# Reordering the hand-written queue at the end of the first pair: last values and output-matrix part five ahead of the norm's multiply and the placing, and the second pair's token sums in order of need

## The chip, the cores and the metric

One core of a Trainium2 chip. The metric is the device time in microseconds (us) of one execution. The kernel is all float32. TensorE (PE) runs the matmuls, VectorE (DVE), ScalarE (ACT) and GpSimd (POOL) the elementwise work, and SyncE (SP) issues most of the DMAs; ACT issues a few.

## The reference, cut to what matters

The input x has 8 sequences of 4096 tokens with 192 features. First a causal convolution over 7 tokens, with softmax weights per head, and then a gated feed-forward network with an RMS norm in front:

```
out = einsum('hk,bskhg->bshg', softmax(weight), windows_of(x))   # 8 heads, 7 taps
x   = out.reshape(32768, 192)
xn  = x / sqrt(mean(x * x, -1) + 1e-6) * rms_g
g   = xn @ w_gate                    # 192 -> 1536
out = (g * sigmoid(g) * (xn @ w_val)) @ w_out   # 1536 -> 192
```

## The kernel before, in words

The tokens are taken in 32 "pairs" of 1024 tokens (two groups g of T = 512). Pair 0 is different from the other 31. It is done with plain products, while the weights are still being converted from their stored form. Pairs 1 to 31 are done with fewer, larger combinations (sums of tokens and sums of weights) and follow one fixed list, `ORDER`. The change concerns only the seam between pair 0 and pair 1, which is passed once.

The program order of each engine is written by hand: the kernel asks for a manual schedule, so each engine executes its instructions in the order in which the Python code emits them, and waits by semaphore for what it needs. For pair 0 the emission is steered by two tables of single letters, each of which advances one generator by a step:

- `s`: one SiLU of a gate product on ACT (L1011). It reads a PSUM bank of half 0 (`ps0` to `ps3`) and writes one of five work tiles.
- `v`: one value step on DVE (L1018). It multiplies a product in a bank of half 1 (`ps4` to `ps7`) by the SiLU tile into `ht`, and gives the bank free.
- `O`: a step of converting an odd part (one, three, five) of the output matrix `wo_sb`. The first step of a part is three DVE operations (L287, L291, L294), the second three ACT operations (L298, L299, L302), the third one DVE operation (L304) and two on POOL (L310, then L311, which writes `wo_sb`). `o` is the same for the even parts.
- `n`: a step of the norm of pair 1. The last of its five steps is a multiply of 128x1536 elements on POOL (L499), which writes `yn`.
- `t`: the placing of pair 1, `place(1)`: eight DMAs that write `yn` to a scratch tensor `xd` in DRAM (L635), four of them issued by SP and four by ACT.
- `w`: sums of the input weights for the later pairs, on POOL (L350, L346).

`START` is played at once, next to pair 0's input products (L1001). `LATER` holds pairs of a time and a letter. Its steps are put into one queue with everything else of pair 0's second stage. The times are only places in that queue (100 is one 512-column product), and the queue is emptied in their order.

The other entries of the queue, with `base` the end of the input products and `c = base + 200`:

- `outer(0, ...)`: pair 0's output products (L1041), 192 instructions on 64 rows of the array each, half 0 and half 1 running beside each other; each shows as two records in the trace. They run over the two token groups g, for each over four blocks j of 128 tokens, and contract over 12 parts f of the hidden features. For g = 0, blocks 0 and 1 lie in banks `ps0` and `ps4`, blocks 2 and 3 in `ps2` and `ps6`. For g = 1 half 0 goes into `ps1` first.
- `part_tap(2, k, j)`: the convolution of pair 2, in PSUM: tap 0 on ACT (L437), taps 1 to 6 on DVE (L445). The three thirds j use banks `ps1`, `ps5` and `ps3` as accumulators; the last tap writes to SBUF and frees the bank. The first two thirds are interleaved, 12 instructions on DVE; the eleventh is the last to read `ps1`.
- `fetch(1)`: four DMAs by SP that read pair 1's tokens from `xd` into `xb` (L648); then `norm(2)` (its square on ACT is L461, its first reduction on DVE L472), and `load(3)`.
- `x_sum(i)`: eleven sums of tokens (L670, DVE) from `xb` into `xc` for pair 1, with sums that build on others.

Pair 1 then begins with products of `xc` and of sums of weights (L757).

Of the kernel before, what the change touches and what calls it, by code (L numbers as in the profile page):

```python
# [19 lines left out]
def kernel(  # L20
# [673 lines left out]
    def put(at, do):  # L694
        heapq.heappush(line, (at, next(tick), do))
# [291 lines left out]
    def plain(hts):  # L987


        groups = [(u, g, f) for u in range(NU) for g in (1, 0) for f in range(NF)]  # L990
        groups[0 : 2 * NF] = [(0, g, f) for f in range(NF) for g in (1, 0)]
        held = {}

        def products():
            for u, g, f in groups:
                if len(hts) <= u:
                    hts.append(big.tile([P, 2, NF, T], F32, name="ht"))
                bks = held[u, g, f] = [free[h].pop(0) for h in range(2)]
                for k in range(KP):
                    for h in range(2):  # L1000
                        nc.tensor.matmul(  # L1001
                            out=bank(h, bks[h])[:], lhsT=wf[u][HALF[h], k * NF + f, :],
                            rhs=xb[HALF[h], g, k, :], start=(k == 0), stop=(k == KP - 1),
                            skip_group_check=True,
                        )
                yield

        def silus():
            for i in groups:
                sg = tiles.pop(0)  # L1010
                nc.scalar.activation(out=sg[:], in_=bank(0, held[i][0])[:], func=AF.Silu)  # L1011
                held[i].append(sg)
                yield

        def values():
            for u, g, f in groups:
                *bks, sg = held.pop((u, g, f))
                nc.vector.tensor_tensor(  # L1018
                    out=hts[u][:, g, f, :], in0=bank(1, bks[1])[:], in1=sg[:], op=ALU.mult
                )  # L1020
                tiles.append(sg)
                for h in range(2):
                    free[h].append(bks[h])
                yield

        return products(), silus(), values()
# [89 lines left out]
    def done(it):  # L1116
# [8 lines left out]

    START = (
        "XxxxxxXDdDdDTDdadTbTaTfbTakTakTakTkbkKkKkKkbkbfpoffpfsicpsvivOpsipisvicpsvpvwsicwpvs"
        "iwpvscwpsiwvpisvicpsvovpwispvswcipvwspsiwOvpsiwvipsvvpswopsvcpsvOnovoOpsonvOpsnoOvnopsoOn"
    )
    LATER = (  # L1130
        (55, "O"), (60, "t"), (163, "s"), (170, "O"), (200, "v"), (294, "v"),
        (463, "w"), (564, "w"), (664, "w"), (764, "w"), (864, "w"), (964, "w"), (1064, "w"),
        (1164, "w"), (1264, "w"),
    )
# [9 lines left out]
    p, sl, v = plain(hts)  # L1144
# [37 lines left out]
    for j in range(len(SIDE)):  # L1182
        put(c + 240 + 700 * (j // 2), functools.partial(part_tap, 2, 0, j))
        for k in range(1, K):
            at = c + 250 + 100 * k + 50 * j if j < 2 else c + 960 + 80 * k
# [3 lines left out]
    later(place(2), c + 2450)  # L1189
    xat = [c + i for i in (1660, 1730, 2060, 2130, 2200, 2270, 2290)]  # L1190
    xat += [c + i for i in (2360, 2370, 2380, 2390)]
    for i, at in enumerate(xat):
        put(at, functools.partial(x_sum, i))
    later(out_sums(), *[base + 2600 + 60 * i for i in range(4 * NM)])
    emit(float("inf"))
# [48 lines left out]
```

## Time and profile before

| | |
|---|---|
| median of 3 runs | 2607.96 us (2606.99 to 2608.02) |
| the profiled execution: its own time | 2610.66 us |
| the profiled execution: span from first to last instruction | 2608.7 us |
| mean granted TensorE clock | 0.997 |
| busy share of the span | PE 99%, DVE 87%, POOL 80%, ACT 62% |
| PE's idle time in the whole run, first 42 us apart | 4.5 us in 4 waits, of which 2.9 us in one |

The page counts an engine as busy while one of its instructions runs. The granted clock is the share of TensorE's full clock that the chip allowed it: at 0.50 a matmul takes twice its time and still counts as busy. Names such as `ps` stand for a whole family of buffers; where the text speaks of `ps1`, the number is from the order of the program.

### The profile page before, as it was taken

What the parts mean: (1) busy time and instruction counts of PE and PEld (TensorE: products, weight loads), DVE (VectorE), ACT (ScalarE), POOL (GpSimd) and SP (SyncE); (2) the same over time, 40 slices, a digit from 0 to 9 for tenths busy, and PEclk for the clock granted to TensorE, in tenths of its full rate; (3) what the DMA queues carried; (4) which work ended last, traced back from release to release, by engine and by line L of the source; (5) the groups of instructions that cost most, each with busy time, mean ns of one, the idle gap of its engine ahead of it and who ended that gap; (6) DMA issues with size and microseconds to landing.
All of it is one profiled execution on the core that took longest, in us unless ns stands there. A gap on an engine that the chain in (4) does not pass through costs nothing.

```text
span 2608.7 us, 60700 instructions
## 1 busy us (share of the span) xinstructions
PE 2575.5 (99%) x23794; PEld 1869.1 (72%) x23794; DVE 2272.6 (87%) x3617; ACT 1618.6 (62%) x2967; POOL 2081.1 (80%) x1693
## 2 busy tenths in 40 slices
PE   6999999999999999999999999999999999999999
PEld 3677777777777766777777777777777777777776
DVE  8988888988888988898888889888888888888875
ACT  5375556765556765557655567655577555676554
POOL 3878788877888777888788887778887888887776
PEclk9999999999999999999999999999999999999999
DMA  6313321323312223213233122232132332232210
GB/s 144 56 39 57 63 47 42 63 39 63 63 35 54 51 51 63 50 39 63 39 63 63 37 52 51 51 63 52 38 61 40 62 63 42 47 60 41 50 38 13
DMA packets 512603, 137.36 MB, mean 53 GB/s; under 512 B 484284, under 2 KB 486844, under 8 KB 512189
## 3 DMA queue, kind: packets, MB, share of 16 engines
q1 hardware_dynamic: 509068, 132.80, 26.7%
q8 instruction: 186, 3.05, 0.5%
q10 hardware_dynamic: 3248, 0.69, 0.1%
q14 instruction: 101, 0.83, 0.1%
HBM read 83.87 MB, written 49.55 MB: 51 GB/s over the span
## 4 chain that ended last, share of the span: by engine, by line
PE 97%; DVE 2%; DMA 0%; ACT 0%; issue 0%; DVEq 0%; SPq 0%; ACTq 0%
PE ps L757 62%; PE ps L889 33%; PE ps L1041 1%; PE ps L1001 1%; DVE xc L304 0%; DMA x<-in_x_dram 0%; DVE ht L1018 0%; DVE y L406 0%; DVE y L421 0%; DVE y L394 0%; PE ps L595 0%; DVE wf L319 0%; ACT xb L615 0%; DVE xc L314 0%; DVE xc L287 0%
## 5 line engine op out<-in xcount | busy, mean ns | idle before, releaser
L757 PE MATMUL ps<-xc,wf 64*128 64x512 f32 x4960 | 1250.0, 592 | 0.0
L757 PEld LDWEIGHTS ps<-xc,wf 64*128 64x128 f32 x4960 | 755.4, 186 | 308.8 <-issue 66.2
L757 PE MATMUL ps<-xb,wf 64*128 64x512 f32 x2480 | 710.4, 589 | 0.0
L801 POOL TENSOR_TENSOR ht<-ht,tile 128x512 f32<-128x512 f32 x298 | 378.8, 1280 | 277.1 <-ACT tile L794 275.1
L708 ACT ACTIVATE tile<-ps 128x512 f32<-128x512 f32 (+1 forms) x677 | 391.0, 593 | 319.5 <-PE ps L757 190.1
L708 ACT ACTIVATE tls<-ps 128x512 f32<-128x512 f32 (+1 forms) x656 | 376.1, 589 | 314.9 <-PE ps L889 192.7
L757 PEld LDWEIGHTS ps<-xb,wf 64*128 64x128 f32 x2480 | 391.9, 187 | 143.6 <-issue 30.7
L708 ACT ACTIVATE ps<-ps 128x512 f32<-128x512 f32 (+1 forms) x651 | 366.9, 578 | 54.0 <-PE ps L889 39.0
L917 POOL TENSOR_TENSOR early<-ht 128x512 f32<-128x512 f32 x279 | 379.4, 1365 | 4.9
L889 PE MATMUL ps<-ht,wo_sb 128*32 128x128 f32 (+2 forms) x5208 | 318.6, 380 | 0.0
L445 DVE SCALAR_TENSOR_TENSOR ps<-xh,tp,ps 128x512 f32<-128x512 f32 x450 | 312.0, 745 | 1.2
L801 POOL TENSOR_TENSOR ht<-ht,tls 128x512 f32<-128x512 f32 x198 | 251.6, 1277 | 76.2 <-ACT tls L794 74.6
L781 DVE TENSOR_TENSOR tile<-ps,tile 128x512 f32<-128x512 f32 x366 | 250.1, 687 | 62.8 <-PE ps L757 56.1
L889 PEld LDWEIGHTS ps<-ht,wo_sb 128*32 128x32 f32 x5208 | 234.2, 110 | 81.5 <-POOL ht L801 23.5
L889 PE MATMUL ps<-ht,x 128*32 128x128 f32 (+2 forms) x4464 | 250.7, 379 | 0.0
L917 POOL TENSOR_TENSOR ht<-ht 128x512 f32<-128x512 f32 x186 | 248.2, 1351 | 0.0
L794 ACT ACTIVATE tile<-tile 128x512 f32<-128x512 f32 x366 | 228.2, 629 | 12.5 <-DVE tile L781 12.5
L889 PEld LDWEIGHTS ps<-ht,x 128*32 128x32 f32 x4464 | 184.6, 110 | 61.1
L781 DVE TENSOR_TENSOR ht<-ps,tile 128x512 f32<-128x512 f32 x322 | 219.1, 681 | 0.1
L781 DVE TENSOR_TENSOR ht<-ps,tls 128x512 f32<-128x512 f32 x298 | 202.7, 680 | 0.0
L889 PE MATMUL ps<-early,x 128*32 128x256 f32 (+2 forms) x3348 | 196.0, 379 | 0.0
L781 DVE TENSOR_TENSOR tls<-ps,tls 128x512 f32<-128x512 f32 x254 | 173.9, 685 | 25.1 <-PE ps L757 23.6
(129 smaller groups left out, 3176.9 us busy)
## 6 DMA issues: line engine op xcount, KB each, us to landing
xb<-xd SPq DMA_DIRECT2D x124, 384.0 KB
xd<-yn SPq DMA_DIRECT2D x244, 96.0 KB
xh<-in_x_dram SPq DMA_DIRECT2D x192, 105.0 KB
out_dram<-o_sb SPq DMA_DIRECT2D x122, 96.0 KB
out_dram<-o_sb SPq DMA_DIRECT2D x62, 128.0 KB
xh<-in_x_dram SPq DMA_DIRECT2D x56, 98.4 KB
out_dram<-o_sb SPq DMA_DIRECT2D x122, 32.0 KB
ht<-in_moe_w_gate_dram SPq DMA_DIRECT2D x12, 192.0 KB
```

What stands on the lines that cost most here:

```text
L445: nc.vector.scalar_tensor_tensor(out=dst, in0=xk, scalar=w, in1=at, op0=ALU.mult, op1=ALU.add)
L708: nc.scalar.activation(out=dst, in_=src, func=AF.Copy, scale=float(s))
L757: nc.tensor.matmul(out=self.new(v, h, True) if first else self.old(v, h), lhsT=wf[self.u][HALF[h], WAT[i], :], rhs=x_op(XOP[i])[HALF[h]], ...
L781: nc.vector.tensor_tensor(out=self.hv(v) if h else t[:], in0=self.old(v, h), in1=t[:], op=plus(s))
L794: nc.scalar.activation(out=t[:], in_=src[:], func=AF.Silu)
L801: engine[eng].tensor_tensor(out=self.hv(v), in0=src, in1=t[:], op=ALU.mult)
L889: nc.tensor.matmul(out=self.bank(b)[i * Q : (i + 1) * Q, at : at + n], lhsT=left, rhs=cols, start=fresh, stop=True, skip_group_check=True, ...
L917: engine[eng].tensor_tensor(out=dst, in0=a, in1=b, op=op)
L1001: nc.tensor.matmul(out=bank(h, bks[h])[:], lhsT=wf[u][HALF[h], k * NF + f, :], rhs=xb[HALF[h], g, k, :], start=(k == 0), stop=(k == KP - 1 ...
L1041: nc.tensor.matmul(out=bank(h, bks[h])[:, w : w + D], lhsT=hts[f // NF][HALF[h], g, f % NF, j * P : (j + 1) * P], rhs=wo_sb[HALF[h], f, :] ...
```

## The change

Two tables are edited; no instruction is added or removed on any engine.

```
-        ...isvicpsvpswopsvcpsvOnovoOpsonvOpsnoOvnopsoOn"
+        ...isvicpsvpswopsvcpsvOnovoOpsonvOpsnoOvnopsoO"
     LATER = (
-        (55, "O"), (60, "t"), (163, "s"), (170, "O"), (200, "v"), (294, "v"),
+        (30, "s"), (35, "v"), (40, "O"), (45, "v"), (50, "O"), (55, "n"), (60, "t"),
         (463, "w"), (564, "w"), (664, "w"), ...
...
     xat += [c + i for i in (2360, 2370, 2380, 2390)]
-    for i, at in enumerate(xat):
+    for i, at in zip((0, 1, 7, 2, 3, 5, 6, 10, 8, 9, 4), xat):
         put(at, functools.partial(x_sum, i))
```

(The first line of `START` is left out above, and the front of its second line is shortened.)

The order that results on each engine:

- DVE: the last two value steps come before L304 of part five; before, they came after it. The eleven token sums keep their places as a group, and inside it stand as 0, 1, 7, 2, 3, 5, 6, 10, 8, 9, 4.
- ACT: the last SiLU comes before the three operations of part five and the four DMA issues; before, it came after them. The square and tap 0 of pair 2 stay behind the DMA issues.
- POOL: L310 and L311 of part five come before L499; before, they came after it.
- PE and SP: the same order as before.

More of the change, by code (lines that the diff above doesn't have):

```diff
@@ L1127 @@
         "XxxxxxXDdDdDTDdadTbTaTfbTakTakTakTkbkKkKkKkbkbfpoffpfsicpsvivOpsipisvicpsvpvwsicwpvs"
-        "iwpvscwpsiwvpisvicpsvovpwispvswcipvwspsiwOvpsiwvipsvvpswopsvcpsvOnovoOpsonvOpsnoOvnopsoOn"
+        "iwpvscwpsiwvpisvicpsvovpwispvswcipvwspsiwOvpsiwvipsvvpswopsvcpsvOnovoOpsonvOpsnoOvnopsoO"
     )
     LATER = (
-        (55, "O"), (60, "t"), (163, "s"), (170, "O"), (200, "v"), (294, "v"),
+        (30, "s"), (35, "v"), (40, "O"), (45, "v"), (50, "O"), (55, "n"), (60, "t"),
         (463, "w"), (564, "w"), (664, "w"), (764, "w"), (864, "w"), (964, "w"), (1064, "w"),
```

## The prediction

> **What bounds the kernel now.** I read the busy row and the chain first: PE is busy for 99% of the span and the chain that ended last is 97% PE. A change that moves no matmul can only touch PE's waits or its clock. So next came PE's waits (engine, line, releaser; total, times, longest):
>
> ```profile
> PE ps L534 <- ACT early L402: 17.6, 2, 16.9
> PE ps L595 <- ACT xc L588: 5.6, 1, 5.6
> PE ps L1041 <- DVE ht L1018: 2.9, 1, 2.9
> ```
>
> The first two lie ahead of pair 0's products and aren't touched. The third is the seam that the change edits. The timelines of DVE, POOL and ACT around it (start, length, engine, line):
>
> ```profile
> 104.54 1.06 DVE L291 TENSOR_SCALAR xc<-xc 128x384 uint32<-128x384 uint32 x1
> 105.52 1.17 DVE L294 TENSOR_SCALAR xc<-tls 128x384 uint32<-128x384 uint32 x1
> 106.62 3.14 DVE L304 SCALAR_TENSOR_TENSOR xc<-tls,xc 128x384 uint32<-128x384 uint32 x1
> 109.68 0.68 DVE L1018 TENSOR_TENSOR ht<-ps,tile 128x512 f32<-128x512 f32 x1
> ...
> 106.44 2.94 POOL L499 TENSOR_TENSOR yn<-y,s 128x1536 f32<-128x1536 f32 x1
> 109.30 1.32 POOL L310 TENSOR_TENSOR xc<-xc,tls 128x384 f32<-128x384 f32 x1
> ...
> 107.16 0.54 ACT L302 ACTIVATE tls<-tls 128x384 f32<-128x384 uint32 x1
> 109.41 2.89 ACTq L635 DMA_DIRECT2D xd<-yn  x4
> 112.35 0.60 ACT L1011 ACTIVATE tile<-ps 128x512 f32<-128x512 f32 x1 [4.65 <-POOL wf L350]
> 112.84 1.90 ACT L437 ACTIVATE ps<-xh,tp 128x512 f32<-128x512 f32 x3
> ...
> 113.58 6.67 DVE L445 SCALAR_TENSOR_TENSOR ps<-xh,tp,ps 128x512 f32<-128x512 f32 x10
> 120.16 1.40 DVE L445 SCALAR_TENSOR_TENSOR y<-xh,tp,ps 128x512 f32<-128x512 f32 x2
> ```
>
> L304 takes 3.14 us because it meets L499 on POOL (beside an idle POOL it took 0.54 at 88.29). The value step behind it starts at 109.68; PE, which wants that step's bank `ps6`, stands from 107.51 to 110.41. The stall costs more than its length; stretches of PE (length, PE busy and records, clock, DMA share and rate):
>
> ```profile
> 107.50:109.60 2.10, 0.01 (x1) 1.00 0.00 0
> 109.60:110.40 0.80, 0.00 (x0) 0.51 0.00 0
> 110.40:116.40 6.00, 5.99 (x38) 0.50 0.61 131
> 116.40:123.00 6.60, 6.60 (x84) 1.00 0.77 175
> ```
>
> From 109.6 to 116.4 half the clock is granted: six microseconds of matmuls do three microseconds' work. The seam costs 2.9 + 3.0 = **5.9 us**, 0.23% of the run; this is the most that the change can win. About 0.2% (5.2 us) is what a measurement of this kernel can tell from no change.
>
> [...] 2.1 us of standing were enough, and half clock lasted 6.8 us. [...] L291 takes 0.36 at 95.46 and 1.06 at 104.54 beside POOL. [...] Here the SiLU at 112.35 stood 4.65 us behind DMA issues.
>
> **The change, part by part, on the profiled execution's clock.**
>
> *Values first.* Up to L294 nothing ahead changes; L294 ends at 106.69. The value step for `ps6` has its SiLU (ended 102.73) and can start at about 106.6; at 0.68 it ends at 107.3. PE wants the bank at 107.36 (the matmul before it starts at 107.19, and they come every 0.16). So this stall goes, with 0.06 to spare. Bounds: 0 to 0.5 us of stall, if DVE slips by half an operation; I take none. The second value step ends at 107.9; its SiLU moves to about 103.3 on an idle ACT, right after the last L1001 product (ended 103.17). That costs nothing.
>
> *Part five before the multiply.* L302 on ACT ends at 107.70 as before, so L310 starts at 107.7 and takes 1.0. L304, now third on DVE, starts at 107.8 and meets L310 as the one at 102.24 did (1.17): it ends at about 109.1. L311 needs it: 109.1 to 110.1. Only then comes L499, alone at 2.9: 110.1 to **113.0**, where it ended at 109.38: 3.6 us later. Bounds 112.6 (L302's end and 1.0 + 1.0 + 2.9) to 113.6. `wo_sb` part five is first needed by matmul record 143, at 107.36 + 86 x 0.081 = 114.3: met with 4 us to spare.
>
> *What stands behind the multiply.* The placing needs `yn`. ACT's four issues took from 109.41 to the next instruction at 112.35, 2.93 us; now 113.0 to 115.9. Behind them in ACT's order is L437, tap 0 of pair 2. It started at 112.84 with the SiLU in front; that is gone, so it starts at about 116.1. The first L445 on DVE followed the first L437's start by 0.74: now 116.8, where it was 113.58. The bank `ps1` is read last by the eleventh L445, which ran from 120.16 to 120.90: now 123.4 to **124.1**.
>
> *When PE wants that bank.* Counting the 384 records of L1041, the first matmul into `ps1` is number 187; it ran at 124.03, 3.1 us after the bank was free, so no wait shows. The one at the old stall is number 57. Without stall and at full clock, 187 comes at 107.36 + 130 x 0.081 = **117.9**. Its bank is free at 124.1. So PE stands for 6.2 us at a new place, and starts record 187 at about 124.2, where it started at 124.03. Both halves of the gain are eaten: PE came 6.1 us earlier and the bank 3.2 us later, against 3.1 us of slack.
>
> *The clock after it.* A stand of 6.2 us is longer than the one that halved the clock. If half clock ends as it did, about 6 us after the restart, 3.0 us are lost behind record 187, which were lost ahead of it before. The price has bounds: 0 if the clock holds, 3.4 if a half-clock stretch of 6.8 us falls wholly on work. I take 3.0.
>
> *Token sums and the rest.* DVE's chain, the fetch, the square and the reductions all shift by about 3.2 us: the last sum ended at 137.7 and now ends at 140.9. PE reaches pair 1 at 124.2 + 16.4 (140.44 less 124.03) + 3.0 = 143.6, where it was 140.1 to 140.4, so the sums are there in any order. Reordering them costs nothing and gains nothing while PE is that late. If the clock held, PE would come at 140.6 and the order would hide up to 0.3 us. SP issues its four placing DMAs and the fetch behind the same multiply: fetch from 116.31 to about 119.9; it took until about 125 to move and would until 129, ahead of the first sum at 133.2. POOL's weight sums start 1.3 us later than their 111.66 and are wanted by later units of pair 1. Nothing of these ends last.
>
> Sum: 124.2 against 124.03 is +0.2, and the half clock moved behind the bank +3.0: **+3.2 us**, on 2608.7 of span and 2610.66 of the profiled execution's own time. The runs' median is 2.7 us under that time; on it I put +3.1: 2611.1.
>
> **The rivals.**
>
> *Half clock only in the new kernel.* The shown runs are 2 to 3.7 us under the profiled execution's time. If this is because their 2.9 us stand, falling otherwise in time, doesn't halve the clock, record 187 starts there at about 121.0 and the new 6.2 us stand costs +3.2 and +3.0: +6.2, 2614.2, slower by 0.24%. It decides once the half-clock loss after exceeds the loss before by 2.0 us. [...] Against it: three runs within 1.0 us don't look like a loss of 3 us that comes and goes.
>
> *The clock holds.* Then the result is +0.2 - 3.0 = -2.8, 2605.2, still no difference that can be told. Against it: 2.1 us sufficed before.
>
> *The bank isn't late.* The gain is the whole 5.9 us, 2602.1, and the sums' new order is what lets PE through at 134.5. It needs `ps1` free at 117.9, and so L437 at about 110, ahead of DMA issues that wait for a multiply ending at 112.6 at the earliest. I see nothing for that but an error in my count of banks.
>
> *It does less than it says.* The `ps6` value step slips and PE still stands there. The restart is set by `ps1` all the same: +3.
>
> **How the numbers follow.** Main case 0.66 (+1.5 to +5), half clock only after 0.17 (+5.2 to +6.5), the clock holds or a shorter chain 0.11 (-3 to +1.5), full gain 0.06. Range: the main case and parts of both neighbours, -0.4 to +6.0, so 2607.6 to 2614.0. Slower by over 0.2%: 0.17; faster: 0.06; within: 0.77.
>
> **What would show it.** Right: no PE wait near 107.5; L499 from about 110 to 113; L437 at about 116; a PE wait of about 6 us at L1041 ended by DVE L445 near 124; clock 0.50 from there for 5 to 7 us; pair 1's first L757 near 143. Wrong: no PE wait at 118, a full clock behind it, or L757 waiting for token sums.

## The result and the profile after

The changed kernel takes 2615.38 us (median of 11 runs, 2614.11 to 2616.81) against 2607.46 us of the kernel before beside it (11 runs, 2606.45 to 2610.98). The medians lie 7.9 us apart, 0.30%; over all these runs the ratio is 1.0026, with a 95% interval of 1.0018 to 1.0034. It is slower, and above the forecast range. The profiled execution of the changed kernel took 2614.11 us with a span of 2612.3 us, which is only 3.6 us over the span of before.

PE's three longest waits in the changed kernel (engine, line, releaser; total, times, longest):

```profile
PE ps L534 <- ACT early L402: 17.1, 1, 17.1
PE ps L1041 <- DVE y L445: 6.8, 1, 6.8
PE ps L595 <- ACT xc L588: 5.6, 1, 5.6
```

The wait of 2.9 us for L1018 is gone. In its place stands one of 6.8 us, ended by L445: the last tap, which gives `ps1` free. DVE's timeline around it (start, length, engine, line):

```profile
104.90 1.17 DVE L294 TENSOR_SCALAR xc<-tls 128x384 uint32<-128x384 uint32 x1
106.00 1.27 DVE L1018 TENSOR_TENSOR ht<-ps,tile 128x512 f32<-128x512 f32 x2
107.20 1.39 DVE L304 SCALAR_TENSOR_TENSOR xc<-tls,xc 128x384 uint32<-128x384 uint32 x1
117.15 6.68 DVE L445 SCALAR_TENSOR_TENSOR ps<-xh,tp,ps 128x512 f32<-128x512 f32 x10 [8.56 <-ACT ps L437]
123.74 1.40 DVE L445 SCALAR_TENSOR_TENSOR y<-xh,tp,ps 128x512 f32<-128x512 f32 x2
```

POOL's:

```profile
107.16 1.01 POOL L310 TENSOR_TENSOR xc<-xc,tls 128x384 f32<-128x384 f32 x1 [1.30 <-ACT tls L302]
108.73 1.00 POOL L311 TENSOR_TENSOR wo_sb<-xc 128x384 f32<-128x384 f32 x1 [0.56 <-DVE xc L304]
109.70 2.86 POOL L499 TENSOR_TENSOR yn<-y,s 128x1536 f32<-128x1536 f32 x1
```

And ACT's, with the DMA issues of its queue:

```profile
106.54 0.54 ACT L302 ACTIVATE tls<-tls 128x384 f32<-128x384 uint32 x1
112.59 3.63 ACTq L635 DMA_DIRECT2D xd<-yn  x4
116.43 1.91 ACT L437 ACTIVATE ps<-xh,tp 128x512 f32<-128x512 f32 x3 [9.34 <-POOL wf L350]
```

Read it from POOL: the multiply L499 now ends at 112.56, the DMA issues on ACT follow at once and hold ACT until 116.43, and DVE stands idle for 8.56 us until tap 0 has run. (This execution reached the seam 0.65 us earlier than the one of before, so its times compare with the prediction's after adding that.) PE in stretches (length, PE busy and records, clock, DMA share and rate):

```profile
107.50:117.70 10.20, 10.20 (x124) 1.00 0.32 67
117.72:121.70 3.98, 0.00 (x1) 1.00 0.30 87
121.70:124.50 2.80, 0.00 (x0) 0.51 1.03 228
124.54:128.50 3.96, 3.96 (x24) 0.50 0.89 177
```

PE runs at full clock through the old stall, stands from 117.72 to 124.54, and then works for 4 us at half clock, which costs 2 us: 24 records in 3.96 us there, 0.165 us each, against 124 in 10.20, 0.082 us each, at full clock. (The half clock lasted 6.8 us, from 121.7 to 128.5; its first 2.8 us fell on the stand.)

The runs of the kernel before lie in two groups, about 2607.6 and about 2610.5: of the 11 above 8 lie in the lower one, and its profiled execution, at 2610.66, is of the upper one.

### The profile page after: what moved, and what is told of

Same layout as the page of the kernel before. It is cut to its first block, busy times and chain, and to the rows that moved or that the text cites. A ratio compares the mean times of both kernels' runs of the same rounds, so it can differ in the third digit from the quotient of the medians.

```text
span 2612.3 us, 60702 instructions
## 1 busy us (share of the span) xinstructions
PE 2575.4 (99%) x23794; PEld 1873.8 (72%) x23794; DVE 2268.1 (87%) x3617; ACT 1617.6 (62%) x2967; POOL 2079.1 (80%) x1693
## 4 chain that ended last, share of the span: by engine, by line
PE 96%; DVE 2%; ACT 1%; issue 0%; DMA 0%; POOL 0%; DVEq 0%; SPq 0%; POOLq 0%; ACTq 0%
PE ps L757 61%; PE ps L889 33%; PE ps L1001 1%; PE ps L1041 1%; DMA x<-in_x_dram 0%; DVE ht L1018 0%; DVE xc L304 0%; DVE y L406 0%; DVE y L421 0%; DVE ps L445 0%; DVE y L394 0%; DVE wf L319 0%; ACT xb L615 0%; PE ps L595 0%; POOL wf L350 0%
## 5 line engine op out<-in xcount | busy, mean ns | idle before, releaser
L757 PE MATMUL ps<-xc,wf 64*128 64x512 f32 x4960 | 1247.6, 592 | 0.4
L757 PEld LDWEIGHTS ps<-xc,wf 64*128 64x128 f32 x4960 | 758.5, 186 | 305.2 <-issue 59.4
L757 PE MATMUL ps<-xb,wf 64*128 64x512 f32 x2480 | 706.9, 589 | 0.0
L757 PEld LDWEIGHTS ps<-xb,wf 64*128 64x128 f32 x2480 | 392.7, 187 | 140.9 <-issue 27.0
L445 DVE SCALAR_TENSOR_TENSOR ps<-xh,tp,ps 128x512 f32<-128x512 f32 x450 | 311.9, 744 | 9.7 <-ACT ps L437 8.6
L889 PE MATMUL ps<-ht,wo_sb 128*32 128x128 f32 (+2 forms) x5208 | 318.6, 380 | 0.0
L889 PEld LDWEIGHTS ps<-ht,wo_sb 128*32 128x32 f32 x5208 | 234.2, 110 | 81.5 <-POOL ht L801 23.5
L889 PE MATMUL ps<-ht,x 128*32 128x128 f32 (+2 forms) x4464 | 250.7, 379 | 0.0
L889 PEld LDWEIGHTS ps<-ht,x 128*32 128x32 f32 x4464 | 184.6, 110 | 61.1
L889 PE MATMUL ps<-early,x 128*32 128x256 f32 (+2 forms) x3348 | 196.0, 379 | 0.0
```

What stands on the lines that cost most here:

```text
L445: nc.vector.scalar_tensor_tensor(out=dst, in0=xk, scalar=w, in1=at, op0=ALU.mult, op1=ALU.add)
L757: nc.tensor.matmul(out=self.new(v, h, True) if first else self.old(v, h), lhsT=wf[self.u][HALF[h], WAT[i], :], rhs=x_op(XOP[i])[HALF[h]], ...
L889: nc.tensor.matmul(out=self.bank(b)[i * Q : (i + 1) * Q, at : at + n], lhsT=left, rhs=cols, start=fresh, stop=True, skip_group_check=True, ...
```

## The experiments

Each of the ten kernels below ran beside the kernel before, on the same chip, in three sessions, whose medians for the kernel before were 2610.40 (49 runs), 2610.01 (49) and 2609.97 (33, on another chip). Most of its runs were in the upper group there: in the first session 40 of 49, with a median of 2610.60, against 2607.67 for the other 9; in the second 31 of 49; in the third 21 of 33. The medians of the two groups agree within 0.1 us in all three, so kernels are best compared group with group.

**The changed kernel again.** No edit.

> The changed kernel once more, beside the others on one chip. Theory A: every run has the 6.8 us stand and 2 to 3.4 us of half clock behind it, one group of runs at 2614 to 2617; the kernel before in two groups, near 2607.6 and near 2610.5, so that the difference of medians depends on how many of before's runs fall in the upper group: 4 to 8 us.

Measured: 2615.79 (13 runs, 2614.64 to 2616.97), ratio 1.0022 (1.0013 to 1.0030), 5.8 us over the median of before, and 8.2 us over the 2607.61 of the lower group. The 6.8 us wait was there again. So the difference of two medians depends on which group the kernel before falls into.

**Filling the stall of the kernel before.** Twelve small matmuls whose results are not used, directly ahead of the one that waits for `ps6` (`idle`, not shown, emits them):

```
+    put(base + 587.5, lambda: idle((1, 0), UPP, 384, 12))   # 12 matmuls, 64 rows x 128 columns
```

> The kernel before, with twelve matmuls of 64 rows x 128 columns (results unused, about 2.5 us) put into PE's order directly ahead of the matmul that stood 2.9 us for ps6. Theory A (the kernel before mostly runs without the half-clock stretch of its profiled execution, and falls into it in a minority of runs): the median stays at about 2607.4, within 0.6 us, and the runs near 2610.6 vanish. Rival B (every run of before pays about 3 us of half clock, and the gap between its profiled execution and its median is something else): every run gets faster by about 3 us, to about 2604.5.

Measured: 2608.32 (13 runs), all within 2607.20 to 2609.15. The upper group is gone, and nothing came down to 2604.5: theory A. Only its "minority of runs" does not hold in these sessions, where most runs of before are in the upper group. The trace's wait of 0.7 us is what the filling left of the old stand: PE went on 8.29 us after its first L1041, against 8.26 in before. The median is 0.7 us over the lower group's; what that is stays open. PE over the old stall, at full clock:

```profile
108.00:111.50 3.50, 2.80 (x28) 1.00 0.00 1
111.50:117.00 5.50, 5.50 (x72) 1.00 0.67 144
```

**The order of the token sums alone**, put into the kernel before:

```
-    for i, at in enumerate(xat):
+    for i, at in zip((0, 1, 7, 2, 3, 5, 6, 10, 8, 9, 4), xat):
```

> The kernel before with only the new order of the eleven token sums. All theories of the seam: no difference (within 0.7 us), since PE reaches pair 1 2.4 us after the last sum in before. If the order of the sums had a cost of its own (a wait of pair 1 on a sum that now comes late), it shows here as a slower run.

Measured: 2610.09 (13 runs, 2607.63 to 2611.86, both groups), ratio 0.9998 (0.9990 to 1.0006): no difference. The two groups, at medians of 2607.98 (6 runs) and 2611.04 (7), lie 0.3 and 0.4 us over those of before. Its profiled execution is of the lower group and shows what that group is: PE's timeline at the seam:

```profile
110.76 2.54 PE L1041 MATMUL ps<-wo_sb,ht 64*128 64x192 f32 x28 [2.89 <-DVE ht L1018]
```

And PE in two stretches around it:

```profile
108.00:111.00 3.00, 0.24 (x2) 1.00 0.00 0
111.00:117.50 6.50, 6.50 (x82) 1.00 0.58 124
```

It is the same stand, 2.89 us for the same step, and the clock stays at 1.00 behind it. In the profiled execution of before the same wait was followed by 6.0 us of work at 0.50.

**Filling the new stall of the changed kernel** with seven matmuls of 128 rows and 512 columns, results not used:

```
+    put(base + 1799.5, lambda: idle((1, 3), slice(0, P), 0, 7))
```

> The changed kernel, with seven matmuls of 128 rows x 512 columns (results unused, about 6.0 us at full clock) put into PE's order directly ahead of the first matmul into ps1, where PE stands 6.8 us. Theory A (stand of 6.8 us plus 2 to 4 us of half clock behind it): the clock stays at 1.00 through the seam, the run gets 2 to 4 us faster than the changed kernel, to about 2611.5 to 2612.5, so about +4.5 us on before. Rival B (the half clock has no part in the loss, it is all stand or something later in the run): stays at 2615.

Measured: 2613.53 (21 runs, 2612.54 to 2614.36), 2.3 us under the changed kernel's 2615.79 (of the second session, on the same chip). It missed its expected band, 2611.5 to 2612.5, by 1 us on the high side; the saving of 2 to 4 us is met. The half clock behind the stand is thus worth 2.3 us. The stand itself remains, filled: PE goes on 23.03 us after its first L1041, against 23.04 in the changed kernel. PE's wait in this kernel, which is the rest of the stand:

```profile
PE ps L1049 <- DVE y L445: 0.6, 1, 0.6
```

PE's timeline, with the filling in it:

```profile
119.43 5.85 PE L1030 MATMUL ps<-wf 128*128 128x512 f32 x13
```

And PE behind it, at full clock:

```profile
126.30:133.00 6.70, 6.67 (x82) 1.00 0.54 110
```

**Values first, and nothing else** (multiply, placing and sums as before):

```
-        (55, "O"), (60, "t"), (163, "s"), (170, "O"), (200, "v"), (294, "v"),
+        (30, "s"), (35, "v"), (40, "O"), (45, "v"), (50, "O"), (60, "t"),
```

> The kernel before with only the last SiLU and the last two value steps moved ahead of L304 of part five; the norm's multiply stays ahead of part five on POOL, the token sums in their old order. Theory A (PE's next bound is ps1, freed by the eleventh L445 behind the DMA issues, in before at about 121): no wait at ps6, but a new one of about 3 us at the first matmul into ps1, ended by L445; same total as before within 1 us, the runs at about 2607.5 or 2610.5 as the half clock falls. Rival B (the value order alone wins the 2.9 us): 2.9 us faster than before in its faster group, about 2604.7.

Measured: 2609.10 (13 runs, 2608.36 to 2612.65), ratio 1.0000 (0.9991 to 1.0008). The medians agree so well only because 10 of these 13 runs are in the lower group, against 18 of 49 of before: that group has a median of 2608.93, 1.3 us over before's 2607.61. The wait changed its name and place and kept its length. From PE's waits:

```profile
PE ps L1041 <- DVE y L445: 2.9, 1, 2.9
```

From DVE's timeline:

```profile
115.07 6.68 DVE L445 SCALAR_TENSOR_TENSOR ps<-xh,tp,ps 128x512 f32<-128x512 f32 x10 [4.09 <-ACT ps L437]
```

PE in two stretches of the profiled execution, which at 2612.50 is of the upper group, with the stand and the half clock behind it:

```profile
117.00:121.50 4.50, 2.53 (x30) 1.00 0.45 121
121.50:128.50 7.00, 6.05 (x38) 0.51 0.72 147
```

With the multiply where it was, the taps are ready 2.9 us too late; part five ahead of the multiply makes it 6.8.

**Tap 0 ahead of the placing**, in the kernel before. The placing moves behind tap 0; the last SiLU, at 163 in the queue, then comes ahead of it too, and nothing else changes:

```
-        (55, "O"), (60, "t"), ...
+        (55, "O"), (445, "t"), ...
```

> The kernel before with one edit alone: tap 0 of pair 2 for ps1 and ps5 ahead of the DMA issues on ACT (placing at 445 and not 60). Values and multiply as in before. Theory A (two bounds in a row, ps6 at the values and ps1 at the taps, and each alone keeps the other's time): the 2.9 us wait at ps6 stays, ps1 is free at about 118, PE passes it later without a wait; total as before within 1 us, in two groups near 2607.6 and 2610.5. Rival B (the taps alone are the bound): about 3 us faster in the fast group, 2604.7.

Measured: 2610.82 (13 runs, 2607.95 to 2611.57, both groups), ratio 1.0006 (0.9998 to 1.0014). The old wait is whole:

```profile
PE ps L1041 <- DVE ht L1018: 2.9, 1, 2.9
```

`ps1` is free at about 118.2 here and PE passes it later without a wait, which alone gives nothing. So there are two bounds in a row, `ps6` at the values and `ps1` at the taps, and removing either one alone gives nothing.

**Tap 0 ahead of the placing in the changed kernel:**

```
-        ... (50, "O"), (55, "n"), (60, "t"),
+        ... (50, "O"), (55, "n"), (445, "t"),
```

> The changed kernel with the placing of pair 1 emitted at place 445 in the queue and not at 60: on ACT, tap 0 of pair 2 for ps1 and ps5 then comes ahead of the four DMA issues, which wait for the multiply. Theory A (the loss comes of ps1, freed late because L437 stands behind the issues): L437 at about 107, L445 from about 108.6, ps1 free at about 116, PE doesn't stand at record 187 (117.4) and keeps its clock; PE reaches pair 1 at about 133.5; about 9 to 10 us faster than the changed kernel, 2604.5 to 2605.5, about 2 to 3 us faster than before. Rival B (the late multiply and late placing are the cost themselves, through the fetch and the token sums): PE passes record 187 and then stands several us at L757 for sums, result no better than before.

Measured: 2611.01 (13 runs, 2608.85 to 2613.29), ratio 1.0004 (0.9995 to 1.0012): 4.8 us better than the changed kernel, half of what theory A said, and no better than before. These runs too lie in two groups, at medians of 2609.4 (6 runs) and 2611.9 (7), 1.7 and 1.3 us over those of before. Theory A's cause is confirmed (no wait at `ps1`), but rival B's wait appears. From PE's waits:

```profile
PE ps L757 <- DVE xc L670: 1.8, 1, 1.8
PE ps L757 <- DVE o_sb L1053: 1.1, 1, 1.1
```

DVE's timeline, the first token sum:

```profile
131.29 0.69 DVE L670 TENSOR_TENSOR xc<-xb 128x512 f32<-128x512 f32 x1 [5.17 <-DMA xb<-xd]
```

SP's timeline, the fetch and the next load of x:

```profile
119.77 2.60 SPq L648 DMA_DIRECT2D xb<-xd  x4
122.48 12.24 SPq L144 DMA_DIRECT2D xh<-in_x_dram  x8
```

The fetch is issued at 119.77, 3.5 us later than in before, because the multiply is late. The taps now end early, which releases the next load of x (L144) at 122.48, right behind the fetch. The first token sum waits 5.17 us for the fetch. That the load slows the fetch is my reading of these lines; I did not run the load by itself.

**The same with the sums in their old order.**

> The changed kernel with tap 0 ahead of the DMA issues (as in e4_tap_first), but the eleven token sums in their old order. In e4 PE waits for sums at L757, so here the order can count. The first sum that PE wants, number 6, stands seventh in both orders; number 10 is eighth in the new one and last in the old. Theory A (the order is worth something only where PE waits for the sums, and then little, since the bank of L1053 behind the sums is wanted soon after): 0 to 1 us slower than e4. Rival B (the new order is what lets PE start): 1.5 to 2.5 us slower than e4.

Measured: 2611.53 (13 runs, 2608.40 to 2612.88) against 2611.01. The 0.5 us is within what these runs scatter, as theory A had it; rival B's 1.5 to 2.5 us is not there. Its profiled execution (2611.95) waits 1.9 us at L757 for a token sum, and has a mean granted clock of 0.997, against 0.999 in that of the kernel above (2609.43).

**All but the late multiply.** Values first, multiply ahead of part five as in before, tap 0 ahead of the placing, new order of the sums. Beside the sums, this is the edit against the kernel before:

```
-        (55, "O"), (60, "t"), (163, "s"), (170, "O"), (200, "v"), (294, "v"),
+        (30, "s"), (35, "v"), (40, "O"), (45, "v"), (50, "O"), (445, "t"),
```

> Values first, the multiply left ahead of part five on POOL, tap 0 of pair 2 for ps1 and ps5 ahead of the DMA issues on ACT, token sums in the new order. Theory A: multiply ends about 109.4, fetch issued from about 116.3, ps1 free by about 117.5, PE wants it at 117.9; no wait of PE over 0.5 us between the input products and pair 1, or at pair 1; full clock through the seam; 2604.5 to 2605.5, about 5 us under the median of before on this chip and 3 us under its fastest group. Rival B (the placing or the fetch still sets the start of pair 1): a wait at L757 for the token sums of 1 us or more, as with the tap moved alone (1.8 and 1.1 us).

Measured: 2606.10 (21 runs, 2605.37 to 2607.18), ratio 0.9987 (0.9981 to 0.9994): 3.9 us under the median of before, 1.5 us under its lower group. This beats both kernels; 2.4 of the 3.9 us are the half clock that 31 of the 49 runs of before beside it pay. The time is 0.6 us over the expected band (later pairs lose 1.2 us, as is told below), but the mechanism is as expected. From DVE's timeline:

```profile
107.95 1.99 DVE L304 SCALAR_TENSOR_TENSOR xc<-tls,xc 128x384 uint32<-128x384 uint32 x1
116.44 1.40 DVE L445 SCALAR_TENSOR_TENSOR y<-xh,tp,ps 128x512 f32<-128x512 f32 x2
```

From ACT's:

```profile
107.75 1.28 ACT L437 ACTIVATE ps<-xh,tp 128x512 f32<-128x512 f32 x2
109.66 3.60 ACTq L635 DMA_DIRECT2D xd<-yn  x4
```

And PE's:

```profile
102.77 31.78 PE L1041 MATMUL ps<-wo_sb,ht 64*128 64x192 f32 x378
```

Tap 0 runs at 107.75, ahead of the DMA issues; `ps1` is free at about 117.2, and PE works through L1041 without a stop.

**The same with the sums in their old order.**

> As e6_values_tap, but the eleven token sums in their old order. Theory A (PE reaches pair 1 after the last sum): no difference from e6, 2605.5 to 2607, no wait at L757. Rival B (PE now comes early enough to need the new order): a wait at L757 for L670 of about 1 us and a median of 2607 or more.

Measured: 2605.91 (21 runs, 2604.77 to 2606.88), ratio 0.9986 (0.9979 to 0.9992), on the other chip, where the lower group of before is at 2607.62; no wait at L757. In none of the three pairs of kernels that differ in the order of the sums alone does it make a difference that can be told.

## Why the prediction was wrong

*The moved wait: right.* It named the new place (the first matmul into `ps1`), the releaser (L445) and the chain (multiply, DMA issues, tap 0, eleven taps). It said 6.2 us; it was 6.8.

*The value steps: right.* PE passes `ps6` without a wait; the two steps run from 106.00 to 107.27, the prediction's times less the 0.65.

*The chain, term by term.* The end of L499 was put at 113.0 and was 112.56 + 0.65 = 113.2. From there to L437 it allowed 3.1 us; it was 116.43 - 112.56 = 3.9. The four issues on ACT took 3.63 from first to last, not the 2.89 taken from before. This term was 0.8 us too small. With it the bank came free 1.0 us later than forecast, at 124.48 + 0.65 = 125.1 and not 124.1. PE was ready a little later too, so the stand is 0.6 us longer.

*The half clock behind the new stand: over-sized.* It was put at 3.0 us and measured at 2.3; in the trace it began 2.8 us before PE went on. That this and the longer stand, -0.7 and +0.6, cancel is luck.

*The kernel before as the base: wrong, and this is the step that failed.* "The clock after it" set 3.0 us of half clock behind the new stand against 3.0 us behind the old one, so that the clock cancelled. That was true of the profiled execution of before and of the upper group, and of no other runs. With the clock held there by filling, the upper group vanishes; the lower group's trace shows the same 2.89 us stand at full clock. The median on which I put +3.1 was that of three runs of the lower group, and 8 of the 11 runs beside the changed kernel are of it too: the 3.0 us behind the new stand had nothing to cancel there. The first rival said exactly this, gave 2614.2, and got 0.17; its +6.2 is right in the cause and still 1.7 us short of the +7.9. The argument against it, that three runs within 1.0 us don't look like a loss that comes and goes, mistook three runs of one group for all. The hint was in plain sight: the profiled execution lay 2.7 us above their median (and 2.6 to 3.7 above the runs, not "2 to 3.7"). Nearly all of the forecast's signs of being right came true: the multiply, L437, the wait and its end, L757 at 143.2 after the 0.65. Only the half clock after the restart was shorter, 4.0 us and not 5 to 7. None of these signs looked at the kernel before, where the error was.

*What can be told.* The forecast took 5.2 us as the least difference that shows. The intervals here are about 0.08% either way, 2.1 us.

*The sum, done again* against before's lower group in the same session, 2615.79 - 2607.61 = 8.2 us: 6.8 - 2.9 = 3.9 for the stands, 2.3 for the half clock (the filling of the changed kernel), and 1.4 in later pairs, of which the next part tells. That makes 7.6; 0.6 us is not accounted for. The stands and the half clock are shown by edits that remove them, the 1.4 us only by laying traces side by side.

*Later pairs: not foreseen.* From the first to the last matmul of L889 the profiled execution of before takes 2410.1 us and that of the changed kernel 2411.5. The excess comes in a few pairs, in steps of up to 0.45 us; the page of the changed kernel shows a trace of it, 0.4 us of idle time before L757 that was 0.0:

```profile
L757 PE MATMUL ps<-xc,wf 64*128 64x512 f32 x4960 | 1247.6, 592 | 0.4
```

The two kernels with before's order of values, multiply and tap (filled stall, sums alone) stay at 2410.1; the others have 2410.6 to 2411.5. It is no chance of one execution: the excess is 1.4 us in the changed kernel, in its repeat and with its stand filled, and 1.2 in the last two kernels of the experiments, in all five with steps of 0.34 to 0.44 us in the 14th, 30th and 31st pair. It goes with the order of the program. The cause is open; no run was aimed at it.

*Token sums: right.* They cost and gain nothing that can be told.

*The rivals.* "The bank isn't late" and "the clock holds" are refuted by the trace after; "it does less than it says" too.

## What to carry to other kernels

Before pricing the removal of a wait, count forward to the next bound on the same engine. Here the next bank had 3.1 us of slack, and the removed wait was 2.9, or 5.9 where the clock was halved behind it; and the edit spent the slack besides by delaying the multiply on which that bank hung. In the changed kernel ACT's DMA issues waited for the multiply, and tap 0 behind them with it: it started at 116.43, after 9.34 us in which ACT computed nothing; put ahead of them, in the kernel with all but the late multiply, it started at 107.75. So put ready work ahead of DMA issues that wait for a slow producer; the two edits that each gave nothing alone gave 3.9 us together, 1.5 of it without the help of the clock. And if a profiled execution lies away from the median of the runs, find out in which way it differs before using its stretches as the base of a difference.

## What the runs showed of the hardware that was not expected

A stand of 2.9 us of PE is followed by half clock in some executions and not in others. In the profiled executions of before (a wait of 2.90 us) and of values first (2.9 us) the clock behind it was 0.50 and 0.51, with 5.99 and 6.05 us of work in that stretch; in that of the sums alone (2.89 us) it stayed at 1.00. By the times of the two groups, 40 of 49 runs of one kernel in one session pay for half clock, 3 of 11 in another, at a price of 2.9 us (2610.60 against 2607.67). A stand of 6.8 us was followed by it in the profiled execution of the changed kernel, and none of that kernel's 24 runs, 2614.11 to 2616.97, lies apart from the others.

At the seam the half clock lasted 6.8 us in the traces of before and of the changed kernel alike: from 109.6 to 116.4, with PE busy for 6.03 us of it, and from 121.7 to 128.5, with PE busy for 3.96. What decides whether a stand of 2.9 us is followed by it was not shown, and why the share of such runs differs so much between sessions stays open.

L304 on DVE took longer where it met L310 or L499 on POOL: 0.54 us beside an idle POOL (before, at 88.29), 1.39 beside L310 (the changed kernel, at 107.20), 1.99 when it came upon L499 1.38 us after that had started, of its 3.06 (all but the late multiply, at 107.95), and 3.14 when it started 0.18 us after it (before, at 106.62); in these last three cases it ended 0.3 to 0.4 us after the POOL instruction. That it waits for POOL is my reading of these times. The value steps (L1018) took 1.27 us for two beside L499, in the kernel with all but the late multiply, and 1.28 beside an idle POOL in the kernel before, at 87.09.
